# A RetNet + mixture-of-experts kernel: down weights in larger DMA packets, up weights read with a step of two, first weights triggered one cast sooner

## The chip, the cores and the metric

The kernel runs on one core of a Trainium2 chip. The metric is the time of one execution on the device in microseconds (us); several executions are timed and the median is given. The profiles hold this one core. "Span" is the length of the profiled execution, about 1.7 us less than its timed length. A "hole" is a stretch in which TensorE stands idle; "half clock" is a stretch in which it was granted half of its full clock (0.50 in the clock records, against 1.00).

## The reference

Retention (attention with a causal decay mask, no softmax) on 8 batches of 8 heads, 576 positions, head size 64, then a dense mixture of 4 experts. Each expert has an up projection (512 to 1024, ReLU) and a down projection (1024 to 512).

```python
ret = scores * Dmat[None]                  # Dmat: gamma_h ** (i - j) for i >= j, else 0
x = np.matmul(ret, v) ... .reshape(4608, 512)
p = domain_probs / (domain_probs.sum(-1, keepdims=True) + 1e-09)
for e in range(4):
    h = np.maximum(x @ w1[e], 0.0)         # w1[e]: 512 x 1024
    out += p[:, e:e + 1] * (h @ w2[e])     # w2[e]: 1024 x 512
```

## The kernel before

The rows of x are done in 9 tiles of 512. Attention of batch 0 opens the kernel, then TensorE works through the 9 tiles, with the attention of the next batch woven in. All weights come from float32 in HBM and are cast to bfloat16 by DMAs that GpSimd issues (the software queue). The raw q, k, v come through the hardware queue of SyncE. The up weights of expert 0, which are needed first, come in two halves; "half one" is hidden units 0 to 511.

```python
    def load_w1(e, part=None):
        if not part:
            w1_sb.append(wpool.tile([128, NDC, F], BF16, tag=f"w1_{e}", name="wt1"))
        f = slice(0, F) if part is None else slice(part * F // 2, (part + 1) * F // 2)
        return nc.gpsimd.dma_start(out=w1_sb[e][:, :, f], in_=moe_w1[e, :, f].rearrange("(dc p) f -> p dc f", p=128))

    def load_w2(e):
        wt2 = wpool.tile([128, NFC, Dm], BF16, tag=f"w2_{e}", name="wt2")
        w2_sb.append(wt2)
        return nc.gpsimd.dma_start(out=wt2, in_=moe_w2[e].rearrange("(fc p) d -> p fc d", p=128))
    # ... cut ...
        def up(ph, e, fc, ts):
            for dc in range(NDC):
                nc.tensor.matmul(ph[:, ts], lhsT=w1_sb[e][:, dc, fc * 128:(fc + 1) * 128],
                                 rhs=xT[:, dc, n0 + ts.start:n0 + ts.stop], start=(dc == 0), stop=(dc == NDC - 1))
    # ... cut: the down projection multiplies hT[:, fc] with w2_sb[e][:, fc] ...
    for x, (hf, u) in enumerate(UNITS):       # the four quarters of batch 0's attention
        # ... cut: transposes T, outputs O of the quarter before ...
        if x < 3:
            a0.cast("k", *UNITS[x + 1], nc.gpsimd)
            a0.cast("q", *UNITS[x + 1], nc.gpsimd)
            if x:
                load_w1(0, x - 1)
            a0.cast("v", *UNITS[x + 1], nc.gpsimd)
        a0.S(hf, u)
        # ...
        a0.kv(hf, u)
    next(tile0)                               # first up matmuls: 256 columns, "half-width"
    a0.O(*UNITS[3])
    next(tile0)
    w20 = load_w2(0)
    # ... cut: the six other weight loads ...
    load_rem(0, w20)                          # 64 remainder rows of batch 0, issued after the first down load landed
    # ... in tile 0: at(20, a0.Trem); at(22, a0.Srem); at(24, a0.Orem)
```

## Time and profile before

| | before |
|---|---|
| time, median of 6 | 565.2 us (564.7 to 565.5) |
| span of the profiled run | 563.2 us |
| TensorE (PE) busy | 98%, mean granted clock 0.999 |
| PE waits for DMA, whole run | 2.1 us, all before 28 us |

The head of the page of the kernel before, its busy line and the chain of work that ended last:

```profile
span 563.2 us, 8301 instructions
PE 553.2 (98%) x3418; PEld 263.7 (47%) x3418; DVE 159.1 (28%) x267; ACT 227.9 (40%) x407; POOL 96.7 (17%) x143
PE 94%; DMA 3%; POOL 1%; SPq 1%; DVE 0%; ACT 0%; issue 0%
```

PE is busy nearly all the time and the chain is PE's own, so only the holes in PE can be filled. The view of waits, PE alone, lists them (total us, times, longest). Three of its seven lines:

```profile
engine line waited for: us in total, times, longest us
PE pt L388 <- POOL qm L378: 1.6, 3, 0.8
PE po L494 <- DMA wt_491<-in_moe_w_dram: 1.4, 1, 1.4
PE ph L465 <- DMA wt_268<-in_moe_w_dram: 0.7, 1, 0.7
```

`wt_268` is the tile of expert 0's up weights, `wt_491` the first down weights. PE in order of time (start, length; L465 is the up projection, L494 the down projection; the lines between are left out):

```profile
17.46 0.61 PE L465 MATMUL ph<-xT,wt_268 128*128 128x256 bf16 x4 [0.68 <-DMA wt_268<-in_moe_w_dram]
18.70 1.91 PE L465 MATMUL ph<-xT,wt_268 128*128 128x256 bf16 x16
21.14 4.93 PE L465 MATMUL ph<-xT,wt_268 128*128 128x256 bf16 x24
27.43 7.08 PE L494 MATMUL po<-wt_491,hT 128*128 128x512 bf16 x32 [1.37 <-DMA wt_491<-in_moe_w_dram]
```

The first up matmuls start at 17.46, once half one has landed. The first down matmul waits 1.37 us for its weights. The DMA view gives the software queue (q0) and the time from issue to landing:

```profile
q0 software_dynamic: 6800, 8.39, 8.7%
wt_268<-in_moe_w_dram POOLq DMA_DIRECT2D x2, 512.0 KB, 6.0
wt_491<-in_moe_w_dram POOLq DMA_DIRECT2D x1, 1024.0 KB, 11.8
wt_496<-in_moe_w_dram POOLq DMA_DIRECT2D x1, 1024.0 KB, 15.1
wt_498<-in_moe_w_dram POOLq DMA_DIRECT2D x1, 1024.0 KB, 21.1
```

### The profile page before, as it was taken

The page shows a single profiled execution, that of the slowest core. Times are in us where ns is not written, and L with a number is a line of the kernel's source. Part 1 is how long each engine was busy: PE and PEld are TensorE (multiplying, and loading weights), DVE is VectorE, ACT ScalarE, POOL GpSimd, SP SyncE. Part 2 cuts the span into 40 slices and gives each one's busy share as a digit, 9 for nine tenths or more (in the row PEclk, how much of TensorE's full clock was granted, in tenths as well). Part 3 has the DMA queues.
Part 4 walks back from the last instruction along what each step waited for, and adds up shares of the span by engine and source line. Part 5 has one row for each costly group of instructions (what it writes and reads, how often), then busy time and mean ns, then how long its engine had stood idle before and what let it go on. Part 6 is the DMA issues. An engine that isn't in the chain of part 4 may idle for free.

```text
span 563.2 us, 8301 instructions
## 1 busy us (share of the span) xinstructions
PE 553.2 (98%) x3418; PEld 263.7 (47%) x3418; DVE 159.1 (28%) x267; ACT 227.9 (40%) x407; POOL 96.7 (17%) x143
## 2 busy tenths in 40 slices
PE   7899999999999999999999999999999999999997
PEld 4544454444444444444444444444444444444443
DVE  6303362243205420442025211432044202220222
ACT  6452334633362236323553336223622353335332
POOL 7511346006010600132010501060000000000000
PEclk9999999999999999999999999999999999999999
DMA  9999999690389025911493048703300100020002
GB/s 236 183 202 200 204 207 224 120 198 1 112 132 168 1 84 106 210 13 38 116 188 72 1 126 156 131 1 99 62 1 1 57 19 1 0 76 1 1 0 76
DMA packets 148150, 53.84 MB, mean 96 GB/s; under 512 B 130540, under 2 KB 142060, under 8 KB 148112
## 3 DMA queue, kind: packets, MB, share of 16 engines
q1 hardware_dynamic: 141168, 44.79, 39.1%
q0 software_dynamic: 6800, 8.39, 8.7%
q8 instruction: 27, 0.44, 0.3%
q10 hardware_dynamic: 144, 0.13, 0.1%
q14 instruction: 11, 0.09, 0.0%
HBM read 45.16 MB, written 9.44 MB: 97 GB/s over the span
## 4 chain that ended last, share of the span: by engine, by line
PE 94%; DMA 3%; POOL 1%; SPq 1%; DVE 0%; ACT 0%; issue 0%
PE po L494 44%; PE ph L465 43%; DMA wt_491<-in_moe_w_dram 2%; PE o L337 1%; PE kvp L236 1%; DMA raw_k<-in_k_dram 1%; PE o L342 1%; SPq L85 1%; POOL km L374 0%; PE orem L353 0%; PE orem L358 0%; PE ptc L284 0%; PE oc L309 0%; POOL wt_268 L119 0%; POOL vm L378 0%; POOL qm L378 0%
## 5 line engine op out<-in xcount | busy, mean ns | idle before, releaser
L484 ACT ACTIVATE hT<-ph 128x512 bf16<-128x512 f32 x288 | 171.6, 597 | 272.7 <-PE ph L465 271.2
L494 PEld LDWEIGHTS <-hT 128*128 128x128 bf16 x1160 | 112.5, 98 | 133.0 <-DMA wt_491<-in_moe_w_dram 1.9
L500 DVE SCALAR_TENSOR_TENSOR acc<-po,probs,acc 128x512 f32<-128x512 f32 (+1 forms) x109 | 81.3, 746 | 227.4 <-PE po L494 220.4
L465 PE MATMUL ph<-xT,wt_496 128*128 128x512 bf16 x288 | 66.8, 379 | 0.0
L465 PE MATMUL ph<-xT,wt_268 128*128 128x512 bf16 (+1 forms) x312 | 64.7, 363 | 1.5 <-DVE xT L316 0.8
L465 PE MATMUL ph<-xT,wt_504 128*128 128x512 bf16 x288 | 66.1, 379 | 0.0
L465 PE MATMUL ph<-xT,wt_500 128*128 128x512 bf16 x288 | 65.8, 379 | 0.0
L494 PE MATMUL po<-wt_491,hT 128*128 128x512 bf16 x288 | 64.5, 379 | 1.4 <-DMA wt_491<-in_moe_w_dram 1.4
L494 PE MATMUL po<-wt_502,hT 128*128 128x512 bf16 x288 | 64.6, 379 | 0.0
L494 PE MATMUL po<-wt_506,hT 128*128 128x512 bf16 (+1 forms) x296 | 64.1, 373 | 0.0
L494 PE MATMUL po<-wt_498,hT 128*128 128x512 bf16 x288 | 64.0, 379 | 0.0
L221 POOL TENSOR_TENSOR km<-raw_k,gk 128x512 bf16<-128x512 f32 x28 | 29.2, 1042 | 138.5 <-PE kvp L236 86.3
L465 PEld LDWEIGHTS <-wt_268 128*128 128x128 bf16 x312 | 30.0, 98 | 32.7 <-issue 0.9
L465 PEld LDWEIGHTS <-wt_500 128*128 128x128 bf16 x288 | 27.4, 98 | 31.5
L465 PEld LDWEIGHTS <-wt_504 128*128 128x128 bf16 x288 | 27.2, 98 | 30.7
L465 PEld LDWEIGHTS <-wt_496 128*128 128x128 bf16 x288 | 27.0, 98 | 28.8
L498 ACT ACTIVATE acc<-po,probs 128x512 f32<-128x512 f32 x36 | 24.7, 687 | 37.6 <-PE po L494 37.6
L223 POOL CAST vm<-raw_v 128x512 bf16<-128x512 f32 x28 | 17.2, 614 | 102.5 <-PE o L337 94.9
L241 ACT ACTIVATE sbd<-kvp 64x256 bf16<-64x256 f32 x56 | 20.9, 372 | 3.7 <-PE kvp L236 3.1
L223 POOL CAST qm<-raw_q 128x512 bf16<-128x512 f32 x28 | 17.1, 610 | 6.8 <-DMA raw_q<-in_q_dram 6.7
L346 DVE TENSOR_TENSOR xT<-o,gq 128x512 bf16<-128x512 f32 x24 | 15.5, 687 | 5.9 <-PE o L342 5.4
L236 PEld LDWEIGHTS <-km 128*128 128x128 bf16 x112 | 8.3, 98 | 6.8 <-issue 0.8
(251 smaller groups left out, 235.8 us busy)
## 6 DMA issues: line engine op xcount, KB each, us to landing
out_dram<-acc SPq DMA_DIRECT2D x35, 256.0 KB, 2.0
raw_k<-in_k_dram SPq DMA_DIRECT2D x32, 256.0 KB, 4.9
raw_q<-in_q_dram SPq DMA_DIRECT2D x32, 256.0 KB, 5.0
raw_v<-in_v_dram SPq DMA_DIRECT2D x32, 256.0 KB, 5.2
wt_268<-in_moe_w_dram POOLq DMA_DIRECT2D x2, 512.0 KB, 6.0
wt_491<-in_moe_w_dram POOLq DMA_DIRECT2D x1, 1024.0 KB, 11.8
wt_496<-in_moe_w_dram POOLq DMA_DIRECT2D x1, 1024.0 KB, 15.1
wt_498<-in_moe_w_dram POOLq DMA_DIRECT2D x1, 1024.0 KB, 21.1
```

The costliest lines, as they stand in the source:

```text
L85: nc.sync.dma_start(out=pairs_of(state[b][n, hf])[:, h], in_=src[b, h, 256 * hf:256 * hf + 256, :].rearrange("h (p j) d -> p h (j d)", j=2))
L221: eng.tensor_tensor(o, i, gk[:, c, :].unsqueeze(2).to_broadcast([128, H, D]), op=MULT)
L223: eng.tensor_copy(o, i)
L236: nc.tensor.matmul(self.kvp[:, p, :], lhsT=flat(self.m["k"][:, n, h, :]), rhs=flat(self.m["v"][:, n, h, :]), start=(n == 0 and i == 0), st ...
L241: nc.scalar.activation(sbd[j:j + 64, n, a:z, j:j + 64], self.kvp[j:j + 64, a:z, j:j + 64], Copy)
L337: nc.tensor.matmul(o[64 * j:64 * j + 64, c * C:(c + 1) * C], lhsT=self.m["v"][:, c, 2 * p + j, :], rhs=self.sT[p][:, j, c, :], start=(c == ...
L346: nc.vector.tensor_tensor(xT[:, p, b * S:b * S + SM], o, gq[:, p, 0:SM], op=MULT)
L465: nc.tensor.matmul(ph[:, ts], lhsT=w1_sb[e][:, dc, fc * 128:(fc + 1) * 128], rhs=xT[:, dc, n0 + ts.start:n0 + ts.stop], start=(dc == 0), s ...
L484: nc.scalar.activation(hT[:, fc, :], ph, Relu)
L494: nc.tensor.matmul(po, lhsT=hT[:, fc, ns * 128:(ns + 1) * 128], rhs=w2_sb[e][:, fc, d:d + w], start=(fc == 0), stop=(fc == NFC - 1))
L498: nc.scalar.activation(a, po, Copy, scale=pe)
L500: nc.vector.scalar_tensor_tensor(a, po, pe, a, op0=MULT, op1=ADD)
```

## The change

A row of w2 is 512 floats, 2 KB. Before, partition p takes rows p, p+128, ..., one packet each. After, it takes rows 2p and 2p+1 of every 256, which lie side by side, so one packet covers both (4 KB) and a load has 512 packets instead of 1024. That permutes the hidden units between partitions, and so the up weights are read with a step of two columns to match. Third, two q casts move from GpSimd to ScalarE and each half of the first up weights is issued one cast sooner.

```diff
-        return nc.gpsimd.dma_start(out=wt2, in_=moe_w2[e].rearrange("(fc p) d -> p fc d", p=128))
+        return nc.gpsimd.dma_start(out=wt2[:, :, :].rearrange("p (fo fi) d -> p fo (fi d)", fi=2),
+                                   in_=moe_w2[e].rearrange("(fo p fi) d -> p fo (fi d)", p=128, fi=2))
@@ up
-                nc.tensor.matmul(ph[:, ts], lhsT=w1_sb[e][:, dc, fc * 128:(fc + 1) * 128],
+                w = w1_sb[e][:, dc, (fc // 2) * 256:(fc // 2 + 1) * 256].rearrange("p (f i) -> p f i", i=2)
+                nc.tensor.matmul(ph[:, ts], lhsT=w[:, :, fc % 2],
@@ start
             a0.cast("k", *UNITS[x + 1], nc.gpsimd)
-            a0.cast("q", *UNITS[x + 1], nc.gpsimd)
             if x:
                 load_w1(0, x - 1)
+            a0.cast("q", *UNITS[x + 1], nc.scalar if x else nc.gpsimd)
             a0.cast("v", *UNITS[x + 1], nc.gpsimd)
```

## The prediction

> **What bounds the kernel now.** TensorE. The page gives PE 553.2 of 563.2 us busy (98%), clock 0.999; the chain of waits is 94% PE. In the timeline 32 matmuls of 128x512 take 6.91 us, 216 ns each, in the up (L465) and the down projection (L494); the 98 ns weight load before each is hidden. The waits view finds few holes in PE: 1.4 us for the first down weights (PE stands from about 26.1 to 27.43 us), 0.7 us for the first half of the first up weights (17.46), 1.6 us in three waits for q casts on POOL, 0.8 us for an xT. All but the last lie in the first 28 us.
>
> **What the change does.**
> 1. Down weights: each of 4 loads goes from 1024 packets to 512 of twice the size; bytes stay. In the DMA view the later up loads (512 packets of the larger kind) land 4.9 to 5.8 us after the load before, down loads 6.7 us. The first down load lands at 27.4, 7.4 us after the second up half (20.0). I estimate 5 to 6 us with larger packets.
> 2. Order: two casts of q leave POOL (0.61 us each) for ACT (0.63 us), and each up half is issued one cast sooner. PE's order does not change. Up half one is issued 0.5 us sooner (10.7), half two and the first down load 0.6 to 0.95 us sooner. For unit 2 ACT is busy with gq until 10.57, so q is ready at 11.2, as before. For unit 3 raw q lands near 13.2, the cast ends near 13.85 instead of 14.3: the transposes start about 0.5 us sooner. ACT's sbd copies slip 0.3 us; I expect PE not to see it.
> 3. Up weights are read with a step of two elements, 1152 weight loads and more. [...] No strided weight load is in this trace. At 216 ns per matmul a 98 ns load may double unseen; only the 48 half-width matmuls (109 ns each, tiles 0 and 1) have no slack. At 130 ns per load those would cost about 1 us; past 216 ns every 10 ns costs 11.5 us.
>
> **On the critical path.** First up matmul 17.46 -> about 16.9 (-0.55). PE will then want the first down weights near 25.5; they should land at 24.5 to 25.2, so the 1.37 us hole goes. Together -1.9 us. The other down loads were already 2 us or more early (landing 39.1 against use at 41.3): their gain is worth nothing, and nobody on PE waits for batch 1's earlier loads.
>
> **Predicted time:** 563.5 us (565.3 - 1.9), 8 in 10 between 562.4 and 565.3. Chances: faster by over 2% 0.01, within 2% 0.95, slower by over 2% 0.04.
>
> **What would show it.** (a) Landing gaps of down weights fall from 6.7 to 5 to 6 us; software queue packets from 6800 to about 4750. (b) PE's wait for the first down weights is gone, or below 0.3 us. (c) The first up matmul starts near 16.9; PE's waits for qm fall by about 0.5. (d) Strided weight loads stay near 98 ns, matmul pitch 216 ns, half-width pitch 109.
>
> **What would make it wrong.** The strided load [...] showing through, first in the half-width matmuls, then everywhere (several us to tens). Larger packets not moving faster because bytes limit the queue (then about 1 us is gained). The ACT cast of unit 3 waiting for raw q and delaying sbd, so that the start gains nothing.

The sum is 0.55 + 1.37 us, about 1.9. That a strided weight load would stay near 98 ns, and so cost nothing, was the author's assumption: no trace held one then. The costs of a slower one are estimates from the 48 half-width matmuls of 109 ns (48 x (130 - 109) ns is about 1 us) and the 1152 weight loads (1152 x 10 ns is 11.5 us).

## The result and the profile after

The changed kernel takes 568.63 us (median of 6, 568.17 to 570.39) against 565.2. The ratio is 1.0066, interval 1.0052 to 1.0079: slower by 3.4 us where I had predicted 1.7 us faster (563.5; the sum in the prediction, 565.3 - 1.9, gives 563.4). A ratio here is the mean time of one kernel's fast runs over that of the other's of the same rounds, so it is not quite the ratio of the quoted medians. The profiled run is the slowest of the six (570.39), so its holes are probably longer than those of a typical run. Its clock is typical: the mean clock of the six runs is 0.993 or 0.994 five times and 0.997 once, which over some 567 us is about 6.8 (from 0.994) and 3.4 us at half speed, an estimate: twice the missing share of the time.

The head of the page and the busy line of the changed kernel:

```profile
span 568.6 us, 8301 instructions
PE 555.3 (98%) x3418; PEld 264.9 (47%) x3418; DVE 159.1 (28%) x267; ACT 228.9 (40%) x409; POOL 95.1 (17%) x141
```

Three lines of PE's waits in the changed kernel (L468 is now the up projection, `wt_267` expert 0's up weights):

```profile
engine line waited for: us in total, times, longest us
PE ph L468 <- DMA wt_267<-in_moe_w_dram: 4.7, 2, 2.5
PE pt L389 <- ACT qm L377: 1.5, 3, 0.8
PE pt L389 <- POOL qm L379: 1.1, 1, 1.1
```

The wait for the first down weights is gone, for PE now comes to them at 32.83, after they landed at 26.87. In its place the up projection waits for its weights twice. PE in order of time shows what the second wait is:

```profile
19.43 0.28 PE L468 MATMUL ph<-xT,wt_267 128*128 128x256 bf16 x1 [2.46 <-DMA wt_267<-in_moe_w_dram]
21.97 0.82 PE L468 MATMUL ph<-xT,wt_267 128*128 128x256 bf16 x3 [2.26 <-DMA wt_267<-in_moe_w_dram]
...
23.91 3.62 PE L468 MATMUL ph<-xT,wt_267 128*128 128x256 bf16 x16
...
28.06 4.93 PE L468 MATMUL ph<-xT,wt_267 128*128 128x256 bf16 x24
32.83 7.07 PE L497 MATMUL po<-wt_491,hT 128*128 128x512 bf16 x32
```

One matmul runs at 19.43, then the second of the same group waits until 21.97. Before, four ran in a row. Half two lands at 21.9 (issued 13.87, 8.05 us to landing), although this matmul reads hidden units 0 to 255 only, which are in half one. The group of 16 then takes 3.62 us instead of 1.91. The table of stretches says why (length, PE busy, granted clock PEclk, DMA share, GB/s), first before, then after:

```profile
20.00:24.00 4.00, 4.00 (x26) 1.00 1.17 183
24.00:28.00 4.00, 2.63 (x13) 1.00 1.17 208
```

```profile
20.00:24.00 4.00, 2.03 (x26) 0.62 1.13 212
24.00:28.00 4.00, 4.00 (x22) 0.52 1.12 211
```

In the second of two long holes the granted clock fell to half speed. The trace's clock records put that from 20.98 to 27.81 us, 6.83 us long. Everything after the first down matmul is as before: it starts 5.40 us later (32.83 against 27.43) and the span is 5.4 us longer. Before, the second up matmul followed the first at a pitch of about 0.11 us, at 17.57, and the work from it to the end of the up group at 26.06 took 8.49 us. So the 5.4 us are: 4.4 us later at that matmul, 2.4 us more for the work that follows (10.86 against 8.49 us), less the 1.37 us hole that is no longer there. In this run half one was late too (its first matmul ran at 19.43 against 17.46), so about 2.0 of the 4.4 us would have come without the false wait; the runs below separate the two.

The DMA lines that answer to those of before:

```profile
q0 software_dynamic: 4752, 8.39, 8.0%
wt_267<-in_moe_w_dram POOLq DMA_DIRECT2D x2, 512.0 KB, 8.1
wt_491<-in_moe_w_dram POOLq DMA_DIRECT2D x1, 1024.0 KB, 11.6
wt_496<-in_moe_w_dram POOLq DMA_DIRECT2D x1, 1024.0 KB, 15.3
wt_498<-in_moe_w_dram POOLq DMA_DIRECT2D x1, 1024.0 KB, 20.3
```

With the issue times (15.22 us for the first down load) it landed at 26.87, 4.9 us after half two; before it was 7.4 us. The larger packets do what they were meant to do. The later down loads show it best (5.7 to 5.8 us after the load before, instead of 6.7 to 6.8), for the first gap also hangs on how late half two is: with the order alone and small packets it was 5.6 us in one profile.

Reading the list of waits that the scheduling layer put into the two programs settles where the second wait comes from, and the traces agree: the weight load that waits for half two's semaphore starts at 22.23 before and at 21.97 after. Before, the first weight load of the up group waits for half one's semaphore, and the load that waits for half two comes at the fifth block of hidden units. After, the second weight load of all waits for half two's semaphore:

```
before: Ldweights wt_268 [waits DMASW0]        after: Ldweights wt_267 [waits DMASW0]
        Matmult   ph<-xT,wt_268 128x256               Matmult   ph<-xT,wt_267 128x256
        Ldweights wt_268                              Ldweights wt_267 [waits DMASW1]   <- half two
```

Why the layer does this is argued only. Per partition the tile is 4 rows (dc) of 1024 columns, and half two is columns 512 to 1023 of every row. As one range of addresses, half two runs from 512 to 4095; the step-of-two read for dc = 0 lies below it, the one for dc = 1 (1024 to 1279) inside. A layer that compares ranges when the read has a step would give just these waits.

### The profile page after: what moved, and what is told of

Read it like the earlier page. It is cut to its first block, busy times and chain, and to the rows that moved or that the text cites. A ratio compares the mean times of both kernels' runs of the same rounds, so it can differ in the third digit from the quotient of the medians.

```text
span 568.6 us, 8301 instructions
## 1 busy us (share of the span) xinstructions
PE 555.3 (98%) x3418; PEld 264.9 (47%) x3418; DVE 159.1 (28%) x267; ACT 228.9 (40%) x409; POOL 95.1 (17%) x141
## 3 DMA queue, kind: packets, MB, share of 16 engines
q0 software_dynamic: 4752, 8.39, 8.0%
## 4 chain that ended last, share of the span: by engine, by line
PE 95%; DMA 2%; SPq 1%; DVE 0%; issue 0%; ACT 0%; POOL 0%
PE ph L468 44%; PE po L497 44%; DMA wt_267<-in_moe_w_dram 1%; PE o L338 1%; PE kvp L237 1%; SPq L85 1%; DMA raw_k<-in_k_dram 1%; PE o L343 1%; PE orem L354 0%; PE orem L359 0%; PE ptc L285 0%; PE oc L310 0%; PE oc L315 0%; POOL km L375 0%; ACT sbd L242 0%
## 5 line engine op out<-in xcount | busy, mean ns | idle before, releaser
L468 PE MATMUL ph<-xT,wt_267 128*128 128x512 bf16 (+1 forms) x312 | 66.9, 372 | 5.5 <-DMA wt_267<-in_moe_w_dram 4.7
L468 PE MATMUL ph<-xT,wt_496 128*128 128x512 bf16 x288 | 66.8, 379 | 0.0
L468 PE MATMUL ph<-xT,wt_504 128*128 128x512 bf16 x288 | 66.2, 379 | 0.0
L468 PE MATMUL ph<-xT,wt_500 128*128 128x512 bf16 x288 | 65.8, 379 | 0.0
L468 PEld LDWEIGHTS <-wt_267 128*128 128x128 bf16 x312 | 30.9, 101 | 37.6 <-DMA wt_267<-in_moe_w_dram 5.1
L468 PEld LDWEIGHTS <-wt_500 128*128 128x128 bf16 x288 | 27.4, 98 | 31.5
L468 PEld LDWEIGHTS <-wt_504 128*128 128x128 bf16 x288 | 27.2, 98 | 30.7
L468 PEld LDWEIGHTS <-wt_496 128*128 128x128 bf16 x288 | 27.0, 98 | 28.8
```

Source lines behind the costliest of these rows:

```text
L468: nc.tensor.matmul(ph[:, ts], lhsT=w[:, :, fc % 2], rhs=xT[:, dc, n0 + ts.start:n0 + ts.stop], start=(dc == 0), stop=(dc == NDC - 1))
```

## The experiments

Theory A: the false wait for half two, and the clock drop that follows, are the loss. Rival B: the new order of issues costs. Rival C: the weight load with a step is slow in itself. "Before" in the same rounds was 565.15 us in the first job, 564.81 in the second and 564.78 in the third.

### The order alone

The kernel before with only the last hunk of the diff above.

> The kernel before with the order part alone (each up half issued one cast sooner, two q casts on ACT); up weights read contiguously, down loads in 1024 packets. Theory A (the time was lost because the strided read makes the second matmul of the first up group wait for the second up half, and the clock drops in that hole): no such wait here; first up matmul waits only for half one; time 564.2 to 565.3 us (0 to 1 us faster than before, because the first down weights still land about 7 us after half two). Rival B (the new order itself is what cost time: [...] one ring lands late): 567 us or more, half one landing near 19 instead of 17.4. Rival C (the strided weight load is slow): same as A here, so this run does not test C.

Measured: 564.66 us (562.99 to 566.12), ratio 0.9991 (0.9975 to 1.0008): no difference can be claimed, and B is refuted as the cause of 3.4 us. The spread of 3.1 us is three times that of before. The profiled run is the slowest of the six, and in it half one came late:

```profile
18.59 0.61 PE L465 MATMUL ph<-xT,wt 128*128 128x256 bf16 x4 [1.78 <-DMA wt<-in_moe_w_dram]
```

Here a single hole of 1.78 us was followed by 3.41 us of half clock (clock records: 19.98 to 23.39), so B's mark (half one landing late) does appear. The recorded clock of each run says how often: it is 0.997 (about 3.4 us at half speed by the same estimate, 3.41 in the profiled one) in the three longest runs, 565.35 to 566.12, and 1.000 in the three shortest, 562.99 to 563.97. So the spread goes with the clock, and where the clock held the order alone was about 1.6 us faster than before. This split was made after the fact. The traces have 16 completion records for each of these loads (what has one record is called a ring here), and at half one the last of the 16 comes 0.84, 2.30 and 1.73 us after the 15th:

```
half one of the up weights: first ring, 15th ring, last ring landed at (us)
before        16.38  16.58  17.42
after         16.45  17.09  19.39
order alone   16.42  16.82  18.55
```

### The wait alone

The kernel before; its second up matmul is made to wait for half two. Nothing of the change is in it.

```diff
-                nc.tensor.matmul(ph[:, ts], lhsT=w1_sb[e][:, dc, fc * 128:(fc + 1) * 128],
+                mm = nc.tensor.matmul(ph[:, ts], lhsT=w1_sb[e][:, dc, fc * 128:(fc + 1) * 128],
                                  rhs=...)
+                if (nt, e, fc, dc, ts.start) == (0, 0, 0, 1, 0):
+                    after(mm, half)          # half: the last load_w1(0, x - 1)
```

> The kernel before (nothing of the change) with only a dependency added: the second matmul of the first up group waits for the second up half. Theory A: PE stands from about 17 to 20 us instead of to 17.5, [...], the half-width matmuls run at half clock; part of the loss is swallowed by the 1.4 us that PE waited for the first down weights anyway; time 565.8 to 568. Rivals B and C: no strided read and no new order here, so 565.2 plus at most 1 us for the plain hole.

Measured: 568.80 us (567.61 to 568.98), ratio 1.0060 (1.0048 to 1.0072), a little above my range. The wait alone makes the whole loss, with packets, strides and order as before. PE in order of time shows the same picture as in the changed kernel, and its clock was at half speed for 6.83 us:

```profile
17.36 0.28 PE L465 MATMUL ph<-xT,wt 128*128 128x256 bf16 x1 [0.44 <-DMA wt<-in_moe_w_dram]
20.26 0.82 PE L465 MATMUL ph<-xT,wt 128*128 128x256 bf16 x3 [2.62 <-DMA wt<-in_moe_w_dram]
...
22.20 3.62 PE L465 MATMUL ph<-xT,wt 128*128 128x256 bf16 x16
```

### The strided read alone

Old order; the down weights in the permuted order but in packets as small as before.

```diff
-        return nc.gpsimd.dma_start(out=wt2, in_=moe_w2[e].rearrange("(fc p) d -> p fc d", p=128))
+        t = wt2[:, :, :].rearrange("p (fo fi) d -> p fo fi d", fi=2)
+        for fi in range(2):
+            i = nc.gpsimd.dma_start(out=t[:, :, fi],
+                    in_=moe_w2[e].rearrange("(fo p fi) d -> p fo fi d", p=128, fi=2)[:, :, fi])
+        return i
@@ up: lhsT with the step of two, as in the change
```

> The kernel before, old order, with the strided read of the up weights alone: the down weights get the matching row order, but in packets as small as before (1024 per load, each load in two pieces). Theory A (false wait for the second up half plus the clock drop; shown sufficient by the run that adds only the wait, 568.8): the second matmul waits for half two, clock near 0.99 over the run and half speed somewhere in 20 to 28 us, time 567.5 to 569.5. Rival C (strided weight loads slow in themselves): over 570, or matmul pitch over 216 ns. If neither (565 or so), the order part of the change is needed for the loss.

Measured: 567.62 us (567.53 to 568.90), ratio 1.0057 (1.0042 to 1.0072). Neither the larger packets nor the order is needed for the loss. PE waited 2.39 us at the second matmul, and half clock lasted 3.41 us:

```profile
20.40 0.82 PE L470 MATMUL ph<-xT,wt 128*128 128x256 bf16 x3 [2.39 <-DMA wt<-in_moe_w_dram]
```

### The change without the false wait

The changed kernel, with the two halves of expert 0's up weights in two tiles. The wait for half two is then back at the fifth block.

```diff
+        t = wpool.tile([128, NDC, F // 2], BF16, tag=f"w1_{e}h{part}", name=f"wt1h{part}")
+        w1_sb[e][part] = t                    # one tile per half
...
-                w = w1_sb[e][:, dc, (fc // 2) * 256:(fc // 2 + 1) * 256].rearrange("p (f i) -> p f i", i=2)
+                w = w1_sb[e][fc // 4][:, dc, (fc % 4 // 2) * 256:(fc % 4 // 2 + 1) * 256].rearrange("p (f i) -> p f i", i=2)
```

> The changed kernel with one thing more: the two halves of the first up weights in two tiles. Theory A: the wait of the second matmul is gone, the clock stays at 1.0, both gains that I predicted appear; time 562.8 to 564.0, about 5 us faster than the changed kernel's 568.6. Rival B: the late ring is still there, 565.5 or more. Rival C: 567 or more, clock full, half-width matmuls slower than 109 ns.

Measured: 565.32 us (564.36 to 566.06), ratio 1.0004 (0.9992 to 1.0015). It is 3.3 us less than the changed kernel, and the clock was 1.0 in the profiled run and two others, so A holds; but my range was 562.8 to 564.0. Two of the five runs, both 566.06 us, had a clock of 0.997; no profile shows why. Rival C is refuted: the strided weight loads take what the plain ones took (98 ns), and 16 half-width matmuls took 1.91 us as before. The view of the up line in this run (min/median/max in ns):

```profile
L474 PEld LDWEIGHTS <-wt x864: 96/98/100, 32.7 to 551.6; 128*128 128x128 bf16 x173
```

About 2 us of the gain that I expected are missing. PE's waits show a new one:

```profile
PE ph L474 <- DMA wt1h<-in_moe_w_dram: 1.1, 1, 1.1
PE ptr L255 <- POOL qrb L236: 0.9, 1, 0.9
```

`qrb` is the bfloat16 copy of the remainder rows of q (64 rows of batch 0), whose raw data come through the hardware queue while the weights still stream.

### The same with the old order

The kernel of the last experiment with the order of before.

> Strided read and the larger down packets with the OLD order, and the two halves of the first up weights kept in two tiles, so that the wait for the second half can't be there. Theory A: first up matmul near 17.5 as before, no second wait, first down weights land about 25 instead of 27.4, their hole of 1.4 us gone; time 563.5 to 564.5. Rival B (order costs): the same, 563.5 to 564.5. Rival C (strided weight load slow): still 567 or more, with the half-width matmuls at a pitch well over 109 ns at full clock.

Measured: 566.36 us (565.95 to 566.58), ratio 1.0018 (1.0005 to 1.0031). This missed my range of 563.5 to 564.5 clearly, so something other than A costs time. There is no false wait (half one landed at 17.74 and four up matmuls ran together from 17.79), but the remainder q made PE wait 1.39 us, and the first down weights still 0.89 us. These were issued at 16.72 us against 15.62 before: the order was the old one, and the raw loads of this run were late from the start (the first v cast at 7.26 against 6.05), which may be part of the miss.

Theory D: the larger software packets hold up the hardware queue, most of whose packets are of 256 bytes here (1670 of the 1718 in the first table below). The DMA view of the stretch from 31 to 45 us, in the kernel before and then in the two-tile kernel with the new order (packets, MB, share of 16 engines):

```profile
q0 software_dynamic: 1831, 2.37, 94.8%
q1 hardware_dynamic: 1718, 0.43, 23.4%
```

```profile
q0 software_dynamic: 1276, 2.55, 95.7%
q1 hardware_dynamic: 1277, 0.32, 17.4%
```

The two queues move nearly the same number of packets in both stretches, 1831 and 1718, then 1276 and 1277. The software queue gains 8% in bytes (2.55 against 2.37 MB) and the hardware queue loses 26% (0.32 against 0.43 MB). The counts fit theory D; how the queues share an engine is not shown.

### Large packets for expert 0 only

The two-tile kernel; experts 1 to 3 load and read their weights as before.

```diff
+        if e:
+            return nc.gpsimd.dma_start(out=wt2, in_=moe_w2[e].rearrange("(fc p) d -> p fc d", p=128))
@@ up
+                if e:
+                    w = w1_sb[e][fc // 4][:, dc, (fc % 4) * 128:(fc % 4 + 1) * 128]
+                else:                          # step of two, as in the change
```

> Two tiles for the first up weights (no false wait), new order, and the larger packets and strided read for expert 0 alone; experts 1 to 3 as before. Theory D (the larger packets starve the hardware queue, [...]: 89 against 121 of its 256-byte packets per us from 31 to 45 us in the traces, and so PE waits 0.9 to 1.4 us for the batch's remainder q): packets of the two queues again about 120 per us, that wait gone; time 563 to 564.5, 0.7 to 2 us below the run with two tiles and large packets everywhere (565.3). If theory D is wrong: 565.3 again.

Measured: 563.38 us (563.06 to 565.41), ratio 0.9982 (0.9970 to 0.9995). This beats both kernels. The same stretch of the DMA view:

```profile
q0 software_dynamic: 1805, 2.34, 93.5%
q1 hardware_dynamic: 1805, 0.45, 24.6%
```

The two queues share about as before the change, and PE's wait for the remainder q is gone. Its only wait for weights is 0.7 us for half one. What the larger packets of expert 0 add to the order is not shown: the five runs here at full clock average 1.3 us under before (563.49 against 564.81), the three such runs of the order alone 1.6 us (563.57 against 565.15).

### The consumer later instead

The two-tile kernel with large packets and the step of two for all experts; only the remainder's place in PE's program changes.

```diff
-            at(20, a0.Trem)
-            at(22, a0.Srem)
-            at(24, a0.Orem)
+            at(23, a0.Trem)
+            at(25, a0.Srem)
+            at(27, a0.Orem)
@@
-            at(25, begin1)
+            at(28, begin1)
```

> Two tiles, new order, strided read and large packets for all experts (565.3 in its first run), with the transposes, scores and outputs of the batch's 64 remainder rows moved 3 groups later in PE's program (about 5 us), so that the remainder q has landed. Theory D (starved hardware queue shows only through that one wait): the wait for the remainder q is gone, the hardware queue is still slow (about 89 packets per us from 31 to 45 us), time 563 to 564.6, like the kernel with large packets for expert 0 alone (563.4). If strided reads or large packets of experts 1 to 3 cost time some other way: 565 or more.

Measured: 563.53 us (563.10 to 564.38), ratio 0.9979 (0.9967 to 0.9992). The hardware queue is as slow as before the move (1275 packets from 31 to 45 us) and the wait for the remainder q is gone. So the larger packets cost time through that one wait, and strided reads and large packets of all experts cost nothing else that can be seen. The size is less sure: no run here had a lowered clock, against two of the five before the move, and without those two the gain is about 1.0 us instead of 1.4.

### Keeping PE busy through the hole: two tries

The changed kernel with extra warm-up matmuls ahead of the first up matmul; the false wait stays.

```diff
         a0.kv(hf, u)
+    warm(24)                                  # second try: warm(14)
     next(tile0)
```

> The changed kernel with 24 extra warm-up matmuls (about 5 us) ahead of the first up matmul, so that PE stays busy while it waits for the second up half; the wait itself stays. Theory: the clock stays at 1.0, the half-width matmuls run at 109 ns again, some 2.5 us come back; first down matmul near 30 instead of 32.8; time 565.5 to 567. If the clock drop cost nothing: 568.2 to 569.

Measured: 567.73 us (567.26 to 569.98), ratio 1.0060 (1.0044 to 1.0075), above my range. The clock stayed at 1.0 in the profiled run (one of the others, 569.98 us, had 0.994), but I had sized the filler by the profiled run of the changed kernel, whose half two came at 21.9. Here it landed at 19.8 and the filler ran to 21.8. So I shortened it.

> The changed kernel with 14 warm-up matmuls (about 3 us, to about 19.8 us) ahead of the first up matmul; with 24 of them PE was kept busy 2 us past the landing of half two (19.8), so that run could not show the gain. Theory: the wait for half two stays, the clock stays at 1.0; first down matmul near 28.2 to 28.8; time 565.5 to 566.8, so about 2 to 3 us of the changed kernel's 568.6 are the clock drop. If the clock drop cost nothing: 568 or more.

Measured: 566.21 us (565.50 to 569.35), ratio 1.0043 (1.0015 to 1.0070): 1.4 us over its own runs of before where the changed kernel was 3.4 us over; clock 1.0 in the profiled run, first down matmul at 28.30. PE in order of time:

```profile
16.54 3.19 PE L135 MATMUL warm_out<-warm_in 128*128 128x512 bf16 x14
19.56 0.91 PE L468 MATMUL ph<-xT,wt 128*128 128x256 bf16 x4
...
21.10 1.91 PE L468 MATMUL ph<-xT,wt 128*128 128x256 bf16 x16
23.54 4.93 PE L468 MATMUL ph<-xT,wt 128*128 128x256 bf16 x24
```

The 16 half-width matmuls are back at 1.91 us. By the medians the half clock was thus about 2.0 us of the loss of 3.4, and the wait itself the rest. By the ratios it is 1.3 us, because one of the four runs took 569.35, and the two intervals overlap, so the times alone do not settle the size. The record shows that this run had a clock of 0.997: about 3.4 us at half speed, so some 1.7 of its extra 3.4 us. It was not profiled.

### Two attempts at more

A short filler of 4 matmuls in the best kernel, `warm(4)` at the same place:

> The same with 4 more warm-up matmuls (0.86 us) ahead of the first up matmul, to bridge the wait for half one, which in some runs is 1 to 2 us long because one of the 16 rings lands late. Where that wait is short it costs nothing to 0.3 us; where it is long, the clock stays up. Theory: the spread of the runs shrinks (order alone: 562.99 to 566.12), median 563 to 564. If the spread is not of the clock: the same spread as the kernel without the warm-up.

Measured: 563.86 us (562.98 to 564.92), ratio 0.9985 (0.9973 to 0.9997). Spread 1.9 us against 2.4 us of the best kernel without it, with 5 and 6 runs: nothing follows. In its profiled run half one landed at 17.93, PE waited 0.38 us for it, and the clock held (1.00 in every stretch up to 550 us).

Half one of the best kernel issued one more cast sooner:

```diff
+            if x == 1:
+                load_w1(0, 0)
             a0.cast("k", *UNITS[x + 1], nc.gpsimd)
-            if x:
-                load_w1(0, x - 1)
+            if x == 2:
+                load_w1(0, 1)
```

> The best kernel so far (two tiles, new order, large packets and stride for expert 0 alone; 563.4) with up half one issued one more cast sooner, before the cast of k for unit 2. It would be issued near 9.7 instead of 11.0 us and land up to 1 us sooner, which takes away PE's wait of 0.7 us for it: 562.5 to 563.4. Rival: its packets compete with the raw q and v loads of unit 3, whose casts already wait 0.7 us for q, and everything shifts back: 563.4 to 565.

Measured: 564.25 us (563.53 to 565.07), ratio 0.9991 (0.9978 to 1.0003). No gain. In its profile half one was issued at 10.27 instead of 11.01 us but landed at 18.28 instead of 17.32, and PE waited 1.17 us for it instead of 0.68. That is what the rival expects, but the raw loads of that run were late from the start (the first v cast at 7.09 us against 6.11), so contention is not shown; what is shown is that issuing sooner did not help.

## Why the prediction was wrong

- **The step that failed: "First up matmul 17.46 -> about 16.9 (-0.55). PE will then want the first down weights near 25.5".** Between these two times the prediction let the up matmuls run through. It looked at the order of PE's instructions, found it unchanged ("PE's order does not change") and went no further. The order was the same; the waits were not. The second matmul of that group got a wait for half two. In the changed kernel's profile it ran at 21.97 instead of about 17.57, and PE came to the first down weights at 32.83. The wait alone gives 568.8 us, the change without it 565.3 us.
- **What it missed next: the clock.** Half clock came in or after the holes before the up matmuls: 6.83 us of it in the profiles of the changed kernel (holes of 2.46 and 2.26 us) and of the wait alone (0.44 and 2.62 us), 3.41 us in those of the stride alone (0.25 and 2.39 us) and of the order alone (1.78 us). None followed the 1.37 us in the kernel before. No run varies the length of the hole alone, so where a limit lies is not shown. With the hole filled, about 2 us came back by the medians (1.3 us by the ratios).
- **"nobody on PE waits for batch 1's earlier loads"** considered batch 1 and not the remainder of batch 0, and supposed that the hardware queue would gain. It lost 26% of its bytes per us from 31 to 45 us to the larger packets (measured in the two-tile kernel). In the changed kernel PE is so late that this does not show; without the false wait it costs 0.9 to 1.4 us of PE's time in the profiles, and moving the consumer brought 1.4 us by the ratios (0.9979 against 1.0004), part of which may be clock.
- **The earlier start did not come.** I put it at 0.55 us, with half one issued at 10.7. In the changed kernel's profile it was issued at 11.18, as before (11.19), and landed late, at 19.39. Even in the best kernel the first up matmul starts at 17.37 against 17.46: the raw k of unit 2 came later in that run (cast at 10.03 against 9.65 us), so half one was issued only at 11.01 against 11.19, and it landed at 17.32. The order alone gives a ratio of 0.9991 over all its runs, no difference that can be claimed.
- **Right:** the packets (4752), the first down load 4.9 us after half two (predicted 5 to 6), the later down loads 5.7 to 5.8 us after the load before (with the issue times, 37.65 after 31.90 us for the second), and the strided load: 98 ns with and without the step, pitch unchanged (at full clock 16 half-width up matmuls take 1.91 us and 32 full-width ones 7.07 us, with and without it).
- **Right by luck:** the hole of 1.37 us is gone in the changed kernel, but because PE comes 5.4 us later; with the wait alone and small packets it is gone too. Only in the two-tile kernels with the new order did the weights come before PE as predicted (in the best one they landed at 25.45 and PE used them at 25.81). The predicted 563.5 us is near what the best kernel reached (563.38), with the false wait and the wait for the remainder q taken away, but its before was 564.81 in that job, so the gain is 1.4 us and not 1.9, and its first up matmul moved by 0.09 us and not 0.55.

What stays open: why the last of the 16 rings lags at half one, by 0.84 to 2.30 us in the table above, and why the clock fell in single runs of kernels without the false wait that were not profiled; and whether the scheduling layer really compares address ranges. A one-tile version laid out half by half, which was built but not run, waits for half two only at the fifth block of hidden units, which fits.

## What to carry to other kernels

When a change touches how a tile is sliced, compare the waits of the two programs, not only the order of instructions: here a strided view picked up a dependency on a load that it does not read (2.26 us of PE's time in the changed kernel's profile, 2.39 us with the stride alone), and separate tiles removed it. A hole in PE cost its own length and then, where the clock fell, more: 2.4 us in the changed kernel's profile, with 6.83 us at half clock. So a hole at the start of dense matmuls is worth filling. Larger packets on one DMA queue took time here from the small packets of another queue that was busy at the same moment (26% of its bytes per us from 31 to 45 us), so it pays to look at that queue's consumers, and to use large packets where the load is urgent (later down loads landed 5.7 to 5.8 us after the load before, instead of 6.7 to 6.8).
